# Strassen sums one at a time, attention at other points, and a softmax of ScalarE passes per head in a fused attention and two-layer kernel

## The chip, the cores and the metric

The kernel runs on one core of a Trainium2 chip. The metric is the device time of one execution in microseconds (us), as the median of several runs. TensorE (PE) multiplies, VectorE (DVE) and ScalarE (ACT) work on tiles, GpSimd (POOL) helps them, SyncE (SP) issues all DMAs in one queue.

## The reference

```python
# attention: B=4, H=8, S=768, D=64; chunks of 32 queries
for c in range(S // 32):
    k_full = concat([mem_k, k[:, :, c*32-16 : c*32+40]])       # 8 + 56 = 64 slots, cut at the ends
    scores = (1 / sqrt(D)) * q_c @ k_full.T
    scores = scores - max(scores, axis=-1)
    a = exp(scores)
    a = a / (sum(a, axis=-1) + 1e-9)
    out[c] = a @ v_full
x = out.transpose(0, 2, 1, 3).reshape(3072, 512)
# layer 1: 512 -> 2048 -> 512
r = maximum(x @ w_in, 0); y = (r * r) @ w_out
# layer 2: 512 -> 2048 -> 512, its own weights
h = y @ w_in2; out = (h * tanh(log1p(exp(h)))) @ w_out2
```

All of it is float32, and the result keeps float32 precision.

## The kernel before

**Steps.** The 3072 tokens are cut into three blocks of 1024, the 2048 hidden columns into eight chunks of 256. One step is one block and one chunk: steps 0 to 23 are layer 1, steps 24 to 47 layer 2, eight steps a block; behind step 47 follows a last stretch. In each step `product` (L478) makes the first matmul of its chunk, from two halves by two halves of both operands, with seven products where eight would be the plain way (Strassen in Winograd's form: S1 to S4 are sums of weight halves, T1 to T4 sums of halves of x). Each operand is split in a rounded part `hi` and a rest `lo`, so a product is six matmuls of 128x512. Results collect in banks a, b, c of PSUM: `u1` is a copy of the first product by ScalarE (L737), `u2`, `u3`, `c22`, `c21`, `c12` are additions on VectorE (L744 to L776), and `gate` (ACT) applies relu and square, or layer 2's function, and casts the result to `hi` (L491); GpSimd subtracts to get `lo` (`split_g`, L492).

**Second matmul.** Between the products of step s stands the second matmul of step s-1. In layer 1 it is eight `unit`s (L533), added to `y` by VectorE. In layer 2 it is seven `product2`s (L568) in pairs of banks 4-5 and 6-7, in the order of `PRODUCTS2`; VectorE adds each to its accumulator `m` (L556, 128x1024), or ScalarE copies it at the first chunk of a block (L579). When a block of layer 2 ends, `combine` adds the seven accumulators up to four outputs: four sums stand together behind the product of T2, three more behind the first three products of the next block's first step, and each output is then stored. The last stretch makes its four outputs in plain form (`last_unit`, L607), in pairs of banks.

**The written order.** The order of instructions on each engine is that of the program text. A step has 15 points, one behind each group of six matmuls (`rest`); at a point waiting stores are issued, one piece of the next weights is loaded, and work that was planned for it is done. `plan_attention` and `plan_w` put such work at offsets in points from a start:

```python
def at(s, i, *work):
    beside.setdefault((s + i // POINTS, i % POINTS), []).extend(work)
...
start, first, period = ((0, 4, 26), (NQ + 1, 10, 19))[sb]
```

**Attention.** It goes in pairs of 128-token tiles, twelve pairs, four for each block. Pairs 0 to 3 come ahead of step 0 (the head), pairs 4 to 7 lie in steps 0 to 7, pairs 8 to 11 in steps 9 to 14. In a pair, `scores` puts two halves of 128x512 in two banks (eight heads of 64 slots each in a half); `softmax` takes the maximum and subtracts it (DVE, L367, L368); `exps` is one exp over 128x512 for each half (ACT, L374); `normalize` sums (DVE, L378), adds 1e-9 and inverts (L380, L381) and multiplies (POOL, L384); `transpose_p` turns the probabilities on TensorE, `copy_pt` copies them to `pt` (ACT, L402), `values` multiplies by v (PE, L414, 128 small matmuls), `copy_x` copies to a stage (ACT, L426), `sums_x` makes T1 to T4 of x (POOL, in the head's last pair DVE), `store_x` stores them to DRAM. A later step loads and splits them again.

**Weights.** Weights come from DRAM in a form that a few passes restore: a rebias on ScalarE (L145), a decode on VectorE (L152), sums on VectorE, a cast to `hi` on ScalarE (L193, L211) and the rest on VectorE (L218); then they are stored to `w_d`, from which each step loads its part. Layer 2's entries are planned from step 8 on: six at one per step, ten more every 9 points from step 17.

**Buffers.** `spare` names the buffers in which the first three accumulators of a block lie (`xt0` to `xt2` or `raw0` to `raw2`, taking turns), while x of the next block is loaded into the others.

## Time and profile before

| | |
|---|---|
| median of 3 runs (lowest, highest) | 1168.34 us (1166.24, 1169.35) |
| the profiled execution: its own time, its span | 1169.24 us, 1167.2 us |
| busy: PE matmul, PE weight load | 1079.9 us (93%), 881.1 us (75%) |
| busy: DVE, ACT, POOL | 896.1 us (77%), 561.5 us (48%), 430.0 us (37%) |
| granted TensorE clock, mean | 0.972 of full speed |
| DMA over the span | 278 GB/s |

The span is the time between the first and the last instruction on the record; the execution's own time has 2 us around it. Busy shares are means over the whole span, over stages with different limits, so that a stretch that matters is read by itself. A clock of 1.00 is 2.4 GHz; a mean between says for how much of a stretch the half level, 1.2 GHz, was granted. A matmul's busy time includes what it takes longer at the half level. A row of a stretch gives its bounds and length, the busy us of PE, PEld, DVE, ACT and POOL in this order with the number of their instructions, the clock, the mean busy share of the DMA engines and what they moved. Steps are named by where their first `product` starts: step 0 at 62.24 us, step 15 at 468.4, step 17 at 509.2, step 26 at 705.8, the last stretch at 1125.2 with step 47 in it.

### The profile page before, as it was taken

To read this page: it belongs to the slowest core of one execution; us is meant where nothing else is said; L and a number is where in the kernel's file an instruction comes from. 1 tells how busy PE (TensorE), PEld (TensorE's weight loads), DVE (VectorE), ACT (ScalarE), POOL (GpSimd) and SP (SyncE) were. 2 spreads that over 40 slices of the span, in tenths; PEclk is the share of its full clock that TensorE was granted. 3 is DMA by queue.
4 is the path that set the end of the run, shared out by engine and by line. 5 is a ranking of instruction groups with operands and counts; after the bars stand their busy time and mean duration, and the time that the engine had idled before them with its cause. 6 is when DMAs were issued, how large, how long until landed. Compare 5 with 4: busy or idle time off the path is not lost.

```text
span 1167.2 us, 19779 instructions
## 1 busy us (share of the span) xinstructions
PE 1079.9 (93%) x7478; PEld 881.1 (75%) x7478; DVE 896.1 (77%) x1164; ACT 561.5 (48%) x879; POOL 430.0 (37%) x333
## 2 busy tenths in 40 slices
PE   6869899898799889999999999999989999799997
PEld 5748688776677778887777778888868888578885
DVE  5586879969666655678998677898878988768886
ACT  2467555555454444557565645444354443253331
POOL 2423223232223323223222244555355545245451
PEclk9999899999989889999999999999999999899998
DMA  9556867777998786869999958989997889867531
GB/s 359 231 193 233 293 214 262 260 277 248 384 320 315 263 292 241 280 237 395 342 338 329 362 218 289 314 304 339 345 309 276 303 304 391 277 207 230 161 128 72
DMA packets 192125, 324.94 MB, mean 278 GB/s; under 512 B 13344, under 2 KB 151072, under 8 KB 188192
## 3 DMA queue, kind: packets, MB, share of 16 engines
q1 hardware_dynamic: 192032, 323.69, 78.0%
q8 instruction: 60, 0.98, 0.3%
q14 instruction: 33, 0.27, 0.1%
HBM read 231.62 MB, written 92.01 MB: 277 GB/s over the span
## 4 chain that ended last, share of the span: by engine, by line
PE 56%; DVE 11%; DMA 7%; ACT 4%; issue 3%; SPq 0%; DVEq 0%; ACTq 0%
PE banks L478 26%; PE banks L568 17%; PE banks L533 10%; DMA w_d<-hi 2%; DVE m L556 2%; DVE y L547 1%; PE banks L414 1%; PE banks L607 1%; DMA w1s<-w_d 1%; DVE ty L632 1%; DVE val L152 1%; DVE r L519 1%; ACT r L497 1%; DMA xt<-xt_d 1%; DMA w2s<-w_d 1%
## 5 line engine op out<-in xcount | busy, mean ns | idle before, releaser
L478 PE MATMUL banks<-x,w1s 128*128 128x512 f32 x2016 | 507.8, 399 | 23.5 <-DVE u L763 7.5
L492 POOL TENSOR_TENSOR g<-r,g 128x512 fp32r<-128x512 f32 x206 | 287.3, 1401 | 537.5 <-ACT g L491 442.6
L478 PEld LDWEIGHTS banks<-x,w1s 128*128 128x128 f32 x2016 | 385.8, 193 | 112.5 <-DVE u L763 9.7
L533 PE MATMUL banks<-g,w2s 128*128 128x512 f32 x1152 | 282.4, 395 | 6.8 <-DVE y L547 5.3
L533 PEld LDWEIGHTS banks<-g,w2s 128*128 128x128 f32 x1152 | 217.2, 190 | 57.7 <-DVE y L547 8.2
L568 PE MATMUL banks<-g,w2s 128*128 128x512 f32 x966 | 241.3, 392 | 9.8 <-ACT m L579 7.6
L568 PEld LDWEIGHTS banks<-g,w2s 128*128 128x128 f32 x966 | 181.2, 189 | 52.2 <-ACT m L579 9.7
L556 DVE TENSOR_TENSOR m<-banks,m 128x1024 f32<-128x1024 f32 x144 | 173.6, 1218 | 34.9 <-PE banks L568 26.3
L491 ACT CAST g<-r 128x512 fp32r<-128x512 f32 x206 | 127.0, 621 | 37.5 <-DVE r L519 30.3
L547 DVE TENSOR_TENSOR y<-banks,y 128x512 f32<-128x512 f32 x168 | 112.0, 682 | 39.0 <-PE banks L533 38.9
L492 POOL TENSOR_TENSOR g<-more,g 128x512 fp32r<-128x512 f32 x55 | 79.7, 1453 | 81.0 <-ACT g L491 66.6
L497 ACT ACTIVATE r<-r 128x512 f32<-128x512 f32 x72 | 45.4, 631 | 69.7 <-DVE r L771 50.1
L501 ACT ACTIVATE r<-r 128x512 f32<-128x512 f32 x48 | 30.4, 632 | 71.4 <-DVE r L771 35.9
L211 ACT CAST hi<-val 128x1024 fp32r<-128x1024 f32 (+1 forms) x32 | 30.4, 949 | 69.5 <-DVE val L156 50.5
L498 ACT ACTIVATE r<-r 128x512 f32<-128x512 f32 x96 | 60.7, 632 | 3.1
L152 DVE TENSOR_SCALAR val<-val 128x512 f32<-128x512 f32 x64 | 38.9, 607 | 26.5 <-ACT val L145 26.4
L414 PE MATMUL banks<-pt,v 64*64 64x32 f32 x1536 | 39.9, 262 | 19.4 <-ACT pt L402 19.0
L218 DVE TENSOR_TENSOR val<-val,hi 128x1024 f32<-128x1024 f32 (+1 forms) x32 | 37.2, 1162 | 25.2 <-ACT hi L211 25.0
L414 PEld LDWEIGHTS banks<-pt,v 64*64 64x64 f32 x1536 | 37.0, 185 | 25.7 <-ACT pt L402 24.8
L737 ACT COPY u<-banks 128x512 f32<-128x512 f32 x48 | 28.1, 585 | 52.0 <-PE banks L478 52.0
L384 POOL TENSOR_TENSOR p<-p,sum 128x512 f32<-128x512 f32 x24 | 28.7, 1215 | 63.3 <-DVE sum L381 25.0
L344 PE MATMUL banks<-k,q 64*32 64x64 f32 x1536 | 37.5, 250 | 13.2 <-DMA k<-k_dram 7.1
(71 smaller groups left out, 999.9 us busy)
## 6 DMA issues: line engine op xcount, KB each, us to landing
w1s<-w_d SPq DMA_DIRECT2D x280, 256.0 KB, 5.4
w2s<-w_d SPq DMA_DIRECT2D x229, 256.0 KB, 5.3
raw<-w_dram SPq DMA_DIRECT2D x64, 512.0 KB, 5.0
w_d<-w1s SPq DMA_DIRECT2D x8, 1792.0 KB, 7.5
x<-xs_d SPq DMA_DIRECT2D x14, 1024.0 KB, 10.7
k<-k_dram SPq DMA_DIRECT2D x24, 512.0 KB, 7.0
v<-v_dram SPq DMA_DIRECT2D x24, 512.0 KB, 8.9
xt<-xt_d SPq DMA_DIRECT2D x21, 512.0 KB, 7.3
```

Source lines behind the costliest of these rows:

```text
L152: nc.vector.tensor_scalar(out=val, in0=val, scalar1=LIMIT, scalar2=-LIMIT * NEGATIVE, op0=ALU.min, op1=ALU.max)
L344: nc.tensor.matmul(out=s4[32 * c:32 * c + 32, j, hp, :], lhsT=q_t[p][r0:r0 + 64, j, hp, 32 * c:32 * c + 32], rhs=k_t[p][r0:r0 + 64, j, hp, ...
L414: nc.tensor.matmul(out=x_ps[par][64 * h2:64 * h2 + 64, o:o + 32], lhsT=v_t[p][j][r0:r0 + 64, h2, a, c, :], rhs=pt_t[p][r0:r0 + 64, h2, j, ...
L478: nc.tensor.matmul(out=ps, lhsT=w[:, a, f:f + 128], rhs=x[:, xi, c, kk, :], start=start and i == 0, stop=stop and i == len(order) - 1, ski ...
L491: nc.scalar.copy(out=g[:, 0], in_=r)
L492: nc.gpsimd.tensor_tensor(out=g[:, 1], in0=r, in1=g[:, 0].bitcast(FP32), op=ALU.subtract)
L497: nc.scalar.activation(out=r, in_=h, func=ACTF.Relu)
L498: nc.scalar.activation(out=r, in_=r, func=ACTF.Square)
L533: nc.tensor.matmul(out=ps, lhsT=w[:, a, blk(f), d % 2 * 128:d % 2 * 128 + 128], rhs=g_t[s, (f, t)][:, c, :], start=i == 0, stop=i == len(o ...
L547: nc.vector.tensor_tensor(out=y, in0=ps, in1=y, op=ALU.add)
L556: engine.tensor_tensor(out=to, in0=in0, in1=in1, op=ALU.add)
L568: nc.tensor.matmul(out=bank(first + d), lhsT=w[:, a, 128 * d:128 * d + 128], rhs=g[:, c, :], start=i == 0, stop=i == 2)
```

## The change

Four things are changed.

1. **Softmax in the steps.** For pairs 4 to 11 VectorE still takes the maximum, then makes `mneg`, the maximum times minus the scale (128x8). ScalarE makes, from PSUM, one exp for each head (64 columns, eight for each half), with `mneg` as bias and the sum of the row as a second result (L389 of the kernel after). The subtraction and the sum on VectorE are left out. Pairs 0 to 3 keep the old form.
2. **Points.** The two halves' exps stand at offsets 3 and 4, the later parts of a pair one or two points later; pairs 4 to 7 come every 25 points where it was 26, pairs 8 to 11 start two points earlier. Layer 2's weights come as seven entries from step 8 on, then nine every 10 points.
3. **Block sums.** `SUMS` lists the seven sums one at a time; each stands behind a product of its own: one behind T2, one behind T1 (these two products change places), one early in the next step, four behind that step's first products. `spare` gives the last block's accumulators `raw0` to `raw2`; `last_unit` uses banks 0 to 3 first.
4. **Head.** In the head the last normalisation and the sums of pair 2 go to VectorE, and four `place_x` calls (which split x into hi and lo) stand earlier.

```diff
@@ -39,10 +39,12 @@
 PRODUCTS = [(A11, B11), (S2, T2), (S1, T1), (A12, B21), (S3, T3), (A22, T4), (S4, B22)]
-PRODUCTS2 = [(A11, B11), (S4, B22), (A12, B21), (S3, T3), (S1, T1), (S2, T2), (A22, T4)]
+PRODUCTS2 = [(A11, B11), (S4, B22), (A12, B21), (S3, T3), (S2, T2), (S1, T1), (A22, T4)]
 STEPS = 2 * NSB * NQ
 OUTPUTS = {T4: (1, 0), B21: (0, 0), T1: (1, 1), B22: (0, 1)}
+SUMS = [(T2, B11), (T3, T2), (T2, T1), (T1, T3), (T4, T3), (B22, T2), (B21, B11)]
@@ -276,7 +278,7 @@
     def spare(sb, i):
-        return f"{('xt', 'raw')[sb % NSB % 2]}{i % 3}"
+        return f"{('xt', 'raw')[(sb - NSB) % 2]}{i % 3}"
@@ -357,31 +359,48 @@
                         )
+    m_neg = {}
     def softmax(p, h2):
         if h2 == 0:
             p_t[p] = pool.tile([128, 2, 8, SLOTS], FP32, tag=f"g{2 + p % 2}" if early(p) else "xt0", name="p")
             r_t[p] = sp.tile([128, 2, 8], FP32, tag="sum", name="sum")
+        s8 = s_ps[p, h2].rearrange("p (a s) -> p a s", a=8)
+        mx = sp.tile([128, 8], FP32, tag="mx", name="mx")
+        nc.vector.tensor_reduce(out=mx, in_=s8, axis=AX.X, op=ALU.max)
+        if early(p):
+            nc.vector.tensor_tensor(
+                out=p_t[p][:, h2], in0=s8, in1=mx.unsqueeze(2).to_broadcast([128, 8, SLOTS]), op=ALU.subtract
+            )
+        else:
+            m_neg[p, h2] = sp.tile([128, 8], FP32, tag="mneg", name="mneg")
+            nc.vector.tensor_scalar(out=m_neg[p, h2], in0=mx, scalar1=-scale, scalar2=None, op0=ALU.mult)
+    def exps(p, h2):
         pr = p_t[p][:, h2]
         s8 = s_ps.pop((p, h2)).rearrange("p (a s) -> p a s", a=8)
-        mx = sp.tile([128, 8], FP32, tag="mx", name="mx")
-        nc.vector.tensor_reduce(out=mx, in_=s8, axis=AX.X, op=ALU.max)
-        nc.vector.tensor_tensor(
-            out=pr, in0=s8, in1=mx.unsqueeze(2).to_broadcast([128, 8, SLOTS]), op=ALU.subtract
-        )
-    def exps(p, h2):
-        pr = p_t[p][:, h2]
-        nc.scalar.activation(out=pr, in_=pr, func=ACTF.Exp, scale=scale)
-    def normalize(p):
-        for h2 in range(2):
-            nc.vector.tensor_reduce(out=r_t[p][:, h2], in_=p_t[p][:, h2], axis=AX.X, op=ALU.add)
+        if early(p):
+            nc.scalar.activation(out=pr, in_=pr, func=ACTF.Exp, scale=scale)
+            return
+        m = m_neg.pop((p, h2))
+        for i in range(8):
+            nc.scalar.activation(
+                out=pr[:, i], in_=s8[:, i], func=ACTF.Exp, scale=scale, bias=m[:, i:i + 1],
+                accum_out=r_t[p][:, h2, i:i + 1],
+            )
+    def normalize(p, engine=nc.gpsimd):
+        if early(p):
+            for h2 in range(2):
+                nc.vector.tensor_reduce(out=r_t[p][:, h2], in_=p_t[p][:, h2], axis=AX.X, op=ALU.add)
         r = r_t[p]
         nc.vector.tensor_scalar_add(out=r, in0=r, scalar1=1.0e-9)
         nc.vector.reciprocal(out=r, in_=r)
         for h2 in range(2):
             pr = p_t[p][:, h2]
-            nc.gpsimd.tensor_tensor(
+            engine.tensor_tensor(
@@ -581,25 +600,19 @@
         add(m, ps, m)
-    def combine(sb, blk, store):
+    def combine(sb, to, other, store=False):
         m = {b: m_t[sb, b] for _, b in PRODUCTS2}
-        if blk == T2:
-            add(m[T2], m[T2], m[B11])
-            add(m[T3], m[T3], m[T2])
-            add(m[T2], m[T2], m[T1])
-            add(m[T1], m[T1], m[T3])
-        else:
-            add(m[blk], m[blk], m[{T4: T3, B22: T2, B21: B11}[blk]])
-        if store:
-            store_y(sb, *OUTPUTS[T1 if blk == T2 else blk], m[T1 if blk == T2 else blk])
+        add(m[to], m[to], m[other])
+        if store and (to, other) in SUMS[3:]:
+            store_y(sb, *OUTPUTS[to], m[to])
     def last_unit(s, n):
         sb = where(s)[1]
         blk = list(OUTPUTS)[n]
         i, t = OUTPUTS[blk]
-        first = (4 + 2 * (pairs[0] % 2), 4 + 2 * ((pairs[0] + 1) % 2), 0, 2)[n]
+        first = (0, 2, 4 + 2 * (pairs[0] % 2), 4 + 2 * ((pairs[0] + 1) % 2))[n]
@@ -645,14 +658,15 @@
             2: lambda: softmax(p, 1),
-            3: lambda: (exps(p, 0), exps(p, 1), load_k(p + 1) if (p + 1) % PSB else None),
-            5: lambda: (normalize(p), load_v(p) if p > PSB else None),
-            11: lambda: transpose_p(p),
-            12: lambda: copy_pt(p),
-            14: lambda: (values(p), load_q(p + 1) if (p + 1) % PSB else None),
-            15: lambda: copy_x(p),
-            16: lambda: sums_x(p, nc.gpsimd),
-            20: lambda: store_x(p),
+            3: lambda: (exps(p, 0), load_k(p + 1) if (p + 1) % PSB else None),
+            4: lambda: exps(p, 1),
+            6: lambda: (normalize(p), load_v(p) if p > PSB else None),
+            12: lambda: transpose_p(p),
+            13: lambda: (copy_pt(p), load_q(p + 1) if (p + 1) % PSB else None),
+            16: lambda: values(p),
+            17: lambda: copy_x(p),
+            18: lambda: sums_x(p, nc.gpsimd),
+            22: lambda: store_x(p),
@@ -720,14 +734,16 @@
             _, sb, j = where(s - 1)
-            final = s == STEPS - 1
-            if (j == NQ - 1 or final) and PRODUCTS2[i][1] == T2:
-                combine(sb, T2, not final)
-            if final and PRODUCTS2[i][1] == T4:
-                for blk in (T4, B22, B21):
-                    combine(sb, blk, False)
-            if sb > NSB and j == 0 and i < 3:
-                combine(sb - 1, (T4, B22, B21)[i], True)
+            blk = PRODUCTS2[i][1]
+            if s == STEPS - 1:
+                for n in {T2: (0,), T1: (1, 2, 3), T4: (4, 6, 5)}.get(blk, ()):
+                    combine(sb, *SUMS[n])
+            elif j == NQ - 1:
+                for n in {T2: (0,), T1: (1,)}.get(blk, ()):
+                    combine(sb, *SUMS[n])
+            elif sb > NSB and j == 0:
+                for n in {B11: (3,), B22: (4,), B21: (5,), T3: (6,)}.get(blk, ()):
+                    combine(sb - 1, *SUMS[n], store=True)
@@ -738,6 +754,8 @@
                 split_g(s - 1, T3, r_ff[s - 1, T3])
+                if where(s - 1)[1] > NSB and where(s - 1)[2] == 0:
+                    combine(where(s - 1)[1] - 1, *SUMS[2])
@@ -814,10 +832,14 @@
             copy_pt(p)
-        def multiply(p):
+        def multiply(p, *others):
             values(p)
+            for other in others:
+                place_x(*other)
             copy_x(p)
-            sums_x(p, nc.vector if p == PSB - 1 else nc.gpsimd)
+            if p == PSB - 1:
+                place_x(p, 0, 3)
+            sums_x(p, nc.vector if p >= PSB - 2 else nc.gpsimd)
@@ -844,16 +866,11 @@
         place_x(0, 3, 7)
-        normalize(3)
+        normalize(3, nc.vector)
         turn(2)
         multiply(2)
-        place_x(1, 0, 3)
-        place_x(1, 3, 7)
         turn(3)
-        multiply(3)
-        place_x(2, 0, 3)
-        place_x(2, 3, 7)
-        place_x(3, 0, 3)
+        multiply(3, (1, 0, 3), (1, 3, 7), (2, 0, 3), (2, 3, 7))
@@ -868,20 +885,22 @@
         for n, e in enumerate(seconds):
-            if n < NQ - 2:
+            if n < NQ - 1:
                 plan_w(NQ + n, 0, e, "Aa|D|d|RS|s|L||||r|l", lambda e, i: round_w2(e, i, "xt2"), split_w2, "val")
             else:
-                n -= NQ - 2
+                n -= NQ - 1
                 hi = (["xt0", "xt1"], ["xt2", "at1"])[n % 2]
                 plan_w(
-                    2 * NQ + 1, 9 * n, e, "Aa|D|d|RS|s|Lr||l",
+                    2 * NQ + 1, 10 * n, e, "Aa|D|d|RS|s|Lr||l",
                     lambda e, i, hi=hi: round_w2(e, i, hi[i]), split_w2, ("val", "at0")[n % 2],
                 )
         for sb in range(NSB - 1):
             p = PSB * (sb + 1)
-            start, first, period = ((0, 4, 26), (NQ + 1, 10, 19))[sb]
-            at(start, 0, *([lambda p=p: load_k(p)] if sb else []), lambda p=p: load_q(p))
+            start, first, period = ((0, 4, 25), (NQ + 1, 8, 19))[sb]
+            at(start, 0, lambda p=p: load_q(p))
+            if sb:
+                at(start, 0, lambda p=p: load_k(p))
```

ScalarE around step 11, from the last gates of step 10 to step 11's `u1`: `pt` is what the product of pair 9 needs, `hi` a weight cast, r and g the gate, `stage` pair 8's x, `u_3965` step 11's `u1`. Before:

```order
L211 CAST hi<-val 128x1024
L497 ACTIVATE r<-r 128x512
L498 ACTIVATE r<-r 128x512
L491 CAST g<-r 128x512
L402 COPY pt<-banks 128x512 x2
L497 ACTIVATE r<-r 128x512
L498 ACTIVATE r<-r 128x512
L491 CAST g<-r 128x512
L426 COPY stage<-banks 128x4x128 x2
L145 ACTIVATE val<-raw 128x512 x2
L737 COPY u_3965<-banks 128x512
```

After (the lines' numbers are those of the kernel after, `u_4049` is the `u1`):

```order
L213 CAST hi<-val 128x1024
L421 COPY pt<-banks 128x512 x2
L516 ACTIVATE r<-r 128x512
L517 ACTIVATE r<-r 128x512
L510 CAST g<-r 128x512
L516 ACTIVATE r<-r 128x512
L517 ACTIVATE r<-r 128x512
L510 CAST g<-r 128x512
L445 COPY stage<-banks 128x4x128 x2
L147 ACTIVATE val<-raw 128x512 x2
L753 COPY u_4049<-banks 128x512
```

The copies of `pt` stood behind the cast and a whole gate; now they follow the cast, ahead of both gates.

VectorE at the first block change of layer 2, from the last addition of step 32 (`r<-banks`) to `u3` of step 33 (`u_7925`); `m<-m` are the sums of `combine`, `u_7855` is `u2`, r and more are the gate's parts. Before:

```order
L776 TENSOR_TENSOR r<-banks,u_7700 128x512
L556 TENSOR_TENSOR m<-banks,m 128x1024
L556 TENSOR_TENSOR m<-m 128x1024 x4
L556 TENSOR_TENSOR m<-banks,m 128x1024
L519 TENSOR_TENSOR r<-r 128x512
L519 TENSOR_TENSOR r<-r,more 128x512
L519 TENSOR_TENSOR r<-r 128x512
L744 TENSOR_TENSOR u_7855<-banks,u_7841 128x512
L519 TENSOR_TENSOR r<-r 128x512
L556 TENSOR_TENSOR m<-m 128x1024 x3
L763 TENSOR_TENSOR u_7925<-banks,u_7841 128x512
```

After (`u_7965` is `u2`, `u_8035` is `u3`; the first of the seven sums stands two rows above the first row here):

```order
L794 TENSOR_TENSOR r<-banks,u_7812 128x512
L575 TENSOR_TENSOR m<-banks,m 128x1024
L575 TENSOR_TENSOR m<-m 128x1024
L575 TENSOR_TENSOR m<-banks,m 128x1024
L538 TENSOR_TENSOR r<-r 128x512
L538 TENSOR_TENSOR r<-r,more 128x512
L538 TENSOR_TENSOR r<-r 128x512
L575 TENSOR_TENSOR m<-m 128x1024
L762 TENSOR_TENSOR u_7965<-banks,u_7950 128x512
L538 TENSOR_TENSOR r<-r 128x512
L575 TENSOR_TENSOR m<-m 128x1024 x3
L781 TENSOR_TENSOR u_8035<-banks,u_7950 128x512
```

The group of four sums is spread: one behind each of two products, one ahead of `u2`, and three, as before, ahead of `u3`.

ScalarE between steps 3 and 4, where pair 6's exps stand ahead of step 4's `u1` (`u_1947`). Before:

```order
L497 ACTIVATE r<-r 128x512
L498 ACTIVATE r<-r 128x512
L491 CAST g<-r 128x512
L374 ACTIVATE p<-p 128x512 x2
L145 ACTIVATE val<-raw 128x512 x2
L737 COPY u_1947<-banks 128x512
L193 CAST w1s<-val 128x768
```

After (`u_1998` is the `u1`):

```order
L516 ACTIVATE r<-r 128x512
L517 ACTIVATE r<-r 128x512
L510 CAST g<-r 128x512
L389 ACTIVATE p,sum<-banks,mneg 128x64 x16
L147 ACTIVATE val<-raw 128x512 x2
L753 COPY u_1998<-banks 128x512
L195 CAST w1s<-val 128x768
```

In the place of two passes stand sixteen, each with a second result, and the same instructions follow them.

## Rows read from the trace of the kernel before

**Rows 1.** Busy time of each engine by stretch, granted clock, DMA share, GB/s

```profile
62.20:468.40 406.20, 369.37 (x3495) 299.17 (x3496) 297.05 (x461) 215.06 (x343) 124.48 (x108) 0.95 0.76 271
468.40:509.20 40.80, 40.80 (x182) 33.78 (x181) 26.16 (x33) 23.18 (x35) 10.31 (x9) 1.00 0.72 249
509.20:705.80 196.60, 187.47 (x806) 150.95 (x805) 162.65 (x242) 113.34 (x172) 54.20 (x39) 0.99 0.91 329
359.10:389.20 30.10, 26.58 (x231) 22.19 (x227) 17.93 (x31) 14.21 (x23) 8.76 (x8) 0.89 0.83 296
705.80:840.10 134.30, 133.99 (x589) 110.03 (x588) 115.31 (x118) 58.30 (x92) 70.31 (x49) 1.00 0.91 325
840.10:865.80 25.70, 21.69 (x85) 16.62 (x84) 21.41 (x20) 12.70 (x18) 11.73 (x7) 0.93 0.74 244
1000.20:1030.00 29.80, 21.98 (x86) 17.02 (x85) 18.11 (x19) 12.85 (x18) 9.35 (x7) 0.89 0.71 235
1125.20:1167.20 42.00, 33.24 (x133) 26.32 (x131) 30.99 (x29) 7.87 (x13) 11.11 (x8) 0.92 0.13 50
```

**Rows 2.** TensorE's timeline: start, us, line, tiles, count, idle time before and releaser

```profile
62.24 7.20 PE L478 MATMUL banks<-x,w1s 128*128 128x512 f32 x18 [3.57 <-ACT x L446]
...
140.63 4.12 PE L414 MATMUL banks<-pt,v 64*64 64x32 f32 x128 [3.25 <-ACT pt L402]
...
382.81 4.12 PE L414 MATMUL banks<-pt,v 64*64 64x32 f32 x128 [3.45 <-ACT pt L402]
...
858.62 4.50 PE L478 MATMUL banks<-x,w1s 128*128 128x512 f32 x12 [3.17 <-DVE u L763]
...
1015.89 2.93 PE L568 MATMUL banks<-g,w2s 128*128 128x512 f32 x6 [6.36 <-ACT m L579]
...
1151.24 11.04 PE L607 MATMUL banks<-g,w2s 128*128 128x512 f32 x36 [3.84 <-DVE m L556]
```

**Rows 3.** Groups by line: count, busy us, mean ns, idle before and releasers

```profile
L374 ACT ACTIVATE p<-p 128x512 f32<-128x512 f32 x24 | 14.8, 629 | 31.5 <-DVE p L368 31.5
L579 ACT COPY m<-banks 128x1024 f32<-128x1024 f32 x21 | 20.9, 1012 | 11.5 <-DVE m L556 6.4 <-DMA out_dram<-m 2.9 <-PE banks L568 2.1
L737 ACT COPY u<-banks 128x512 f32<-128x512 f32 x48 | 28.1, 585 | 52.0 <-PE banks L478 52.0
L368 DVE TENSOR_TENSOR p<-banks,mx 128x512 f32<-128x512 f32 x24 | 16.6, 692 | 2.2 <-PE banks L344 0.8 <-DVE mx L367 0.2
L378 DVE TENSOR_REDUCE sum<-p 128x8 f32<-128x512 f32 x24 | 15.4, 677 | 1.9 <-ACT p L374 1.7
L380 DVE TENSOR_SCALAR sum<-sum 128x16 f32<-128x16 f32 x12 | 2.4, 196 | 0.4
```

**Rows 4.** Timelines of TensorE and of ScalarE at the start of step 4

```profile
170.52 4.24 PE L478 MATMUL banks<-x,w1s 128*128 128x512 f32 x18
...
172.93 0.58 ACT L737 COPY u<-banks 128x512 f32<-128x512 f32 x1
```

**Rows 5.** ScalarE's timeline in steps 11 and 13

```profile
377.39 1.05 ACT L211 CAST hi<-val 128x1024 fp32r<-128x1024 f32 x1 [3.20 <-DMA w_d<-hi]
...
382.18 1.07 ACT L402 COPY pt<-banks 128x512 f32<-128x512 f32 x2
...
418.31 1.22 ACT L145 ACTIVATE val<-raw 128x512 f32<-128x512 f32 x2 [5.85 <-DMA w_d<-val]
```

**Rows 6.** Timelines of VectorE and of GpSimd at the first block change

```profile
840.22 5.01 DVE L556 TENSOR_TENSOR m<-m 128x1024 f32<-128x1024 f32 x4
...
851.22 6.74 DVE L556 TENSOR_TENSOR m<-m 128x1024 f32<-128x1024 f32 x3
...
847.74 4.71 POOL L492 TENSOR_TENSOR g<-r,g 128x512 fp32r<-128x512 f32 x3 [7.98 <-ACT g L491]
```

**Rows 7.** ScalarE's timeline at the second block change

```profile
1019.28 1.01 ACT L579 COPY m<-banks 128x1024 f32<-128x1024 f32 x1 [2.92 <-DMA out_dram<-m]
```

**Rows 8.** VectorE's timeline, its last addition

```profile
1162.32 1.23 DVE L556 TENSOR_TENSOR m<-banks,m 128x1024 f32<-128x1024 f32 x1 [1.49 <-PE banks L607]
```

## The prediction

> **What bounds the kernel now.** I read the stretches by engine first [rows 1]. TensorE sets the time: in steps 26 to 32 it is busy for 133.99 of 134.30 us, 19.19 us a step, and in steps 15 and 16 for 40.80 of 40.80, 20.40 us a step. So a change pays only where TensorE stands idle, or works at the half level of its clock (1.2 GHz) behind an idle stretch. The other rows of the group show where that is: steps 0 to 14 take 406.2 us at a mean clock of 0.95; steps 17 to 25 take 196.6 us where eight steps at 20.40 and one at 19.19 make 182.4, so 14 us too many; the steps in which layer 2 passes from one token block to the next take 25.7 and 29.8 us, 6.5 and 10.6 too many; and the last stretch takes 42.0 us. Then I read TensorE's timeline for what ended each wait [rows 2]: the start of layer 1 waits for a cast of x (3.57 us), three attention products wait for the transposed probabilities `pt` (3.25 and 3.45 us; the third row, at 420 us, is like them), the two block changes wait 3.17 for `u3` on VectorE and 6.36 for a copy of ScalarE, the end waits 3.84 for VectorE. The 128 matmuls of a product that waited take 4.12 us, at the half clock: in the step of the second of them (359 to 389 us) the mean clock is 0.89, so that of 30.1 us some 6.6 us ran at half speed [rows 1], which lose 3.3 us of work on top of the wait.
>
> **The change, part by part.** Times are against the profiled execution, 1169.24 us with a span of 1167.2; the median of the runs, 1168.34, is 0.9 lower.
>
> *Softmax, prices.* Per head half VectorE loses the subtraction (692 ns) and the sum (677) and gains one 128x8 multiply, for which the 128x16 scalar row stands, 196 [rows 3]. That is 1.17 us less, sixteen times, 18.8 us. ScalarE does eight passes over 64 columns, each with a sum as second result, for one pass over 512 of 629 ns. No row shows such a pass. Below: copies from PSUM take 585 ns for 512 columns and 1012 for 1024 [rows 3], so 0.83 ns a column and 158 fixed, 211 ns for 64. Above: as much as the whole 512 pass, 629. I take the middle, 0.42, as if the sum were a second small instruction: 3.4 us a half, 6.7 a pair against 1.26, so 5.5 more per pair and 44 us for eight. ScalarE is busy for 215 of 406 us there [rows 1], so most of it has room; what counts is what stands behind the passes in ScalarE's queue. The small VectorE work of `normalize` now waits for the last pass, and that holds VectorE up about as long as the dropped sums took: I count no gain for VectorE, except in steps 5 and 6, where the passes follow `gate` in ScalarE's idle middle.
>
> The Trainium skill, "ScalarE: Activation LUTs", section "What ACT_TABLE_LOAD costs", speaks against cutting the pass: a pass with a per-partition bias costs about 280 ns plus 0.833 a column, and neighbours overlap by 93, which is an estimated 240 ns a pass and 1.9 us a half. It gives no price for the sum; with 240 ns the two losses (c) and (f) below vanish and the total falls by 3.5 us; no row shows the pass itself.
>
> (a) Head: the last pair's normalisation and pair 2's block sums leave GpSimd for VectorE, and three casts move ahead of the last stage copy, so layer 1's first product starts some 2 us before its 62.24 [rows 2]; but the sums of pair 3 now follow one more cast, and in step 0 the sixteen passes (6.7 us) delay the next use of VectorE. Net 0.8 gained, from 3 lost to 3.5 gained.
> (b) Step 2: the product comes one group of 1.36 us (20.40/15) later behind its copies, so the wait of 3.25 falls to 1.9, and some half-clock time with it: 3 us, from 1.4 to 4.6.
> (c) Pair 6: its sixteen passes end step 3's queue, ahead of the rebias passes and of step 4's `u1`, which starts at 172.93 where its step starts at 170.52 [rows 4], 2.4 us in. 5.5 us later it is at 7.9; the fourth product needs its bank at 6.8. Lost 1.5, from 0 to 5.
> (d) Steps 5 and 6: 2.4 us less of VectorE work in two steps that are full of it: 3 gained, from 0 to 4.7. (e) Step 7 waits for the x that pair 7 stores; its sums stand one point earlier: 1.5, from 0 to 3.5.
> (f) Pair 8: as (c), ahead of step 10's `u1` and of three copies of `y`: lost 2, from 6 lost to 1 gained.
> (g) Step 11: pair 9 moves two points forward, its product keeps its place. In ScalarE's queue `pt` stood behind a whole gate, at 382.18 [rows 5]; now it follows the cast at 377.39, so it is there at about 379.5 and the wait of 3.45 all but ends. 6.6 with the clock; I take 5, since that cast itself waited 3.20 for a store. From 1 to 6.6.
> (h) Step 13: the copies of pair 10 stood behind a rebias pass that waited 5.85 us for a store [rows 5]; now they are queued a step earlier, ahead of it. 6.5 with the clock, I take 5, from 1 to 6.6.
> (i) Steps 17 to 25: one of ten weight entries goes to step 14, which has room, and the others come every 10 points, not 9. VectorE loses some 8 us there (three passes for each half, the sums, two splits), but three casts, where it was two, now fall just ahead of a `u1`. 2 gained, from 3 lost to 6 gained.
> (j) First block change. Before, four sums follow each other behind one product (5.01 us) and three more (6.74) stand ahead of `u3` [rows 6]. Now one follows each of two products, one stands ahead of `u2` and three ahead of `u3`. VectorE reaches the next step some 4 us earlier. How long a sum takes depends on its neighbour: 1.25 us where GpSimd stood idle, 2.25 beside GpSimd's splits, which themselves took 1.57. With 1.25 each nothing waits, and 6.5 is gained; with 2.25, `u3` is ready about 1.4 us earlier only. I take 4, from 1.4 to 6.5.
> (k) Second change: besides, the outputs of the last block go to `raw`, not to `xt`, from which the block before is still being stored: the copy at 1019.28 waited 2.92 us for that store [rows 7]. 10.6 at most, 5.5 at least (it becomes as long as the other change less 1.4); I take 8.
> (l) End: the first two of the four last products use banks 0 to 3, which nothing holds, so the wait of 3.84 [rows 2] and its half clock go: 48 matmuls at 0.228 (19.19/84) are done some 7 us sooner. The sums and additions on VectorE are then late next: its last addition, which ended at 1163.55 (1162.32 plus 1.23) [rows 8], ends 5 to 6 us earlier. 5.5, from 3.8 to 6.
>
> The swap of two products needs the split of T2 a product earlier; in the clean steps it stands ready, and I count nothing (a miss would cost one split, 1.6 us, in each block change). The stores of (k) move on SP's queue with their sums; weights wait behind them there, but are loaded a step ahead: nothing. The loads of k, v and q move by a point or two; nothing, with the bounds of (f) as cover.
>
> Sum: 0.8+3-1.5+3+1.5-2+5+5+2+4+8+5.5 = 34.3, so 1134.9 for this execution and 1134 for the median. The terms' half ranges, taken as independent, make 10 us, so this case alone lies between 1122 and 1146.
>
> **The rivals.** *The passes cost 0.63 us.* 3.4 us more per pair; wholly on the path in pairs 6 and 8, half so in 4 and 5: 10 us, and pairs 9 and 10 lose the half of (g) and (h): 1149. For: the sum may be a slow second instruction. Against: no ScalarE row has more than some 0.2 us fixed.
> *The stalls of steps 11 and 13 come back.* They hang on stores of 5.85 and 3.20 us in a stretch whose DMA share is 0.83 [rows 1]; a faster TensorE asks for more. (b), (g) and (h) go: 1147.
> *The sums stay slow.* A sum took 2.25 us beside GpSimd's splits against 1.25 without [rows 6]. Here all seven may fall beside splits in both changes; then `u3` is late again, and (j) and (k) keep their low ends, 1.4 and 5.5: 1139. The Trainium skill, "SBUF — State Buffer", section "Who interferes with whom", makes this the rule: a VectorE instruction with two SBUF inputs and a GpSimd one that reads SBUF exclude each other for a whole instruction; by that rule every sum beside a split is slow, and the two prices in the rows agree with it.
> *Slower.* Every pair's passes lie on the path: a gate, `u1` or `pt` stands behind them and TensorE waits for all of it. At 0.42 that is 44 us for eight pairs against 37.8 of gains without (c) and (f): 1174. It decides from 0.41 us a pass on. For: pairs 6 and 8. Against: ScalarE's 191 idle us in that stretch, and four pairs whose passes precede a gate that waits for VectorE anyway.
>
> **How the numbers follow.** Forecast 0.59, dear passes 0.12, stalls that return 0.14, slow sums 0.08, slower 0.07. The low end, 1118, is the forecast's with half of its (a), (g), (h) and (j) at their best; the high end takes in the first three rivals and a mix of them: 1153. A measurement tells 0.3% (3.5 us) from no change: slower takes 0.06 of its rival, no change 0.03 between the two sides, and faster the rest, 0.91.
>
> **What would show it.** Right: no wait of TensorE over 1 us at the last products and at the second block change; `pt` not the releaser in steps 11 and 13; passes of 0.4 us apart; `u1` late in steps 4 and 10. Wrong: passes of 0.6 us or more, steps 0 to 14 no shorter than 400 us in sum, or a block change still above 24 us.

## The result and the profile after

The changed kernel takes 1127.3 us (median of 4 runs, 1126.7 to 1130.86), the kernel before 1167.29 beside it; the ratio is 0.9662, with an interval of 0.9636 to 0.9688. Forecast were 1134, between 1118 and 1153. The profiled execution took 1127.79 us, with a span of 1126.0 against 1167.2.

The stretches by engine, after, in the columns of [rows 1]: steps 0 to 14, steps 17 to 25, the first block change, the last stretch:

```profile
61.40:453.50 392.10, 361.82 (x3495) 294.17 (x3496) 285.38 (x459) 244.00 (x585) 124.98 (x107) 0.96 0.80 285
495.80:680.30 184.50, 183.10 (x805) 150.62 (x804) 156.34 (x230) 110.78 (x168) 54.85 (x39) 1.00 0.93 334
814.70:836.90 22.20, 19.67 (x86) 15.62 (x85) 19.55 (x18) 12.26 (x18) 11.56 (x8) 1.00 0.63 213
1088.50:1126.00 37.50, 30.06 (x133) 24.57 (x131) 31.23 (x29) 7.76 (x13) 12.07 (x8) 0.96 0.15 56
```

Steps 0 to 14 took 406.2 us and take 392.1; steps 17 to 25 took 196.6 and take 184.5, which is eight times 20.40 and 19.19 plus 2; the block changes fell from 25.7 and 29.8 to 22.2 and 22.1, the end from 42.0 to 37.5. ScalarE is busy for 244 us in the first stretch, where it was 215, and VectorE for 285, where it was 297.

By the terms of the prediction, in us, from the starts of the steps in the traces; the last column is a second profile of the changed kernel, from the runs below:

| stretch | terms | forecast | after | second profile |
|---|---|---|---|---|
| head, step 0 | (a) | -0.8 | -1.7 | -1.2 |
| steps 1 to 4 | (b), (c) | -1.5 | -1.9 | -4.0 |
| steps 5 to 8 | (d), (e) | -4.5 | -3.8 | -3.1 |
| steps 9 to 16 | (f), (g), (h) | -8.0 | -5.9 | -0.3 |
| steps 17 to 25 | (i) | -2.0 | -12.1 | -12.6 |
| step 33 | (j) | -4.0 | -3.5 | -2.2 |
| step 41 | (k) | -8.0 | -7.7 | -6.3 |
| last stretch | (l) | -5.5 | -4.5 | -4.5 |
| span | | -34.3 | -41.2 | -34.3 |

One profile is a weak measure of steps 9 to 14: in the four profiles (of the kernel before and of three runs below) whose code there is that of before, they take 165.9 to 173.0 us. The profile of before, at 173.0, is the longest of the four.

TensorE's waits after, as in [rows 2] (two products of attention, the two block changes, the end):

```profile
135.21 0.30 PE L433 MATMUL banks<-pt,v 64*64 64x32 f32 x2 [1.48 <-ACT pt L421]
...
180.36 0.30 PE L433 MATMUL banks<-pt,v 64*64 64x32 f32 x2 [1.40 <-ACT pt L421]
...
830.96 3.02 PE L497 MATMUL banks<-x,w1s 128*128 128x512 f32 x12 [2.53 <-DVE u L781]
...
987.41 3.02 PE L497 MATMUL banks<-x,w1s 128*128 128x512 f32 x12 [2.50 <-DVE u L781]
1107.52 11.04 PE L620 MATMUL banks<-g,w2s 128*128 128x512 f32 x48
```

No attention product waits over 1.5 us for `pt`, ScalarE's copy at the second block change is no releaser any more, and the 48 matmuls at the end follow without a wait. `u3` is what both block changes still wait for.

A pass of the new softmax and the start of the next, in ScalarE's timeline of step 0 (sixteen follow each other):

```profile
76.99 0.31 ACT L389 ACTIVATE p<-banks,mneg 128x64 f32<-128x64 f32 x1
77.20 0.19 ACT L389 ACTIVATION_READ_ACCUMULATOR p<-banks,mneg 128x1 f32 x1
77.29 0.30 ACT L389 ACTIVATE p<-banks,mneg 128x64 f32<-128x64 f32 x1
```

It is two instructions, the exp and a read of the sum, which overlap: the next pass starts 0.29 to 0.30 us after the last, sixteen take 4.7 us. I had put 0.42 a pass.

### The profile page after: what moved, and what is told of

The parts are those of the page before. It is cut to its first block, busy times and chain, and to the rows that moved or that the text cites. A ratio compares the mean times of both kernels' runs of the same rounds, so it can differ in the third digit from the quotient of the medians.

```text
span 1126.0 us, 19983 instructions
## 1 busy us (share of the span) xinstructions
PE 1061.0 (94%) x7478; PEld 871.6 (77%) x7478; DVE 884.1 (79%) x1154; ACT 589.1 (52%) x1119; POOL 429.0 (38%) x327
## 4 chain that ended last, share of the span: by engine, by line
PE 70%; DVE 12%; ACT 6%; DMA 6%; issue 5%; POOL 1%; SPq 0%; DVEq 0%; ACTq 0%; POOLq 0%
PE banks L497 31%; PE banks L587 17%; PE banks L552 16%; DVE m L575 3%; PE banks L433 3%; PE banks L346 2%; DMA w_d<-hi 2%; ACT p L389 1%; DVE r L538 1%; DMA k<-k_dram 1%; ACT r L517 1%; DMA xt<-xt_d 1%; ACT r L516 1%; DVE y L566 1%; DVE ty L645 1%
## 5 line engine op out<-in xcount | busy, mean ns | idle before, releaser
L497 PE MATMUL banks<-x,w1s 128*128 128x512 f32 x2016 | 500.9, 395 | 21.7 <-DVE u L781 8.7
L497 PEld LDWEIGHTS banks<-x,w1s 128*128 128x128 f32 x2016 | 380.4, 190 | 107.4 <-DVE u L781 10.4
L346 PEld LDWEIGHTS banks<-k,q 64*32 64x32 f32 x1536 | 32.7, 122 | 24.1 <-issue 20.6
L158 DVE SCALAR_TENSOR_TENSOR val<-raw,val 128x512 uint32<-128x512 uint32 x64 | 49.0, 765 | 2.2
L403 POOL TENSOR_TENSOR p<-p,sum 128x512 f32<-128x512 f32 x22 | 25.9, 1197 | 58.8 <-DVE sum L400 39.4
```

The costliest lines, as they stand in the source:

```text
L158: nc.vector.scalar_tensor_tensor(out=vb, in0=low, scalar=29, in1=vb, op0=ALU.logical_shift_right, op1=ALU.bitwise_or)
L346: nc.tensor.matmul(out=s4[32 * c:32 * c + 32, j, hp, :], lhsT=q_t[p][r0:r0 + 64, j, hp, 32 * c:32 * c + 32], rhs=k_t[p][r0:r0 + 64, j, hp, ...
L497: nc.tensor.matmul(out=ps, lhsT=w[:, a, f:f + 128], rhs=x[:, xi, c, kk, :], start=start and i == 0, stop=stop and i == len(order) - 1, ski ...
```

## The experiments

The steps are compared by their starts in the profiles; ratios are to the kernel before on the same chip, whose median was 1164.9, 1163.9 and 1164.2 us in the three sets.

**One part of the change alone.** Four kernels are the kernel before with one part each; the fourth part of the change, the head, was not run alone.

```diff
+SUMS, PRODUCTS2, combine, done, last_unit, spare and the early sum as in the change
```

> The kernel before with the block sums one at a time, the swapped products, the other order of banks at the end and the last block's accumulators in raw; attention, softmax, weights and head as before. My theory, that the terms add: step 33 falls by 3.5 us, step 41 by 7.7, the last stretch by 4.5, the rest stays, so 15.7 us in all: about 1151.6 us. Rival, that these stretches gained because the steps before them came at other times: less than half of it, 1160 or above.

Measured: 0.9861 (0.9833 to 0.989), 1149.96 us. Step 33 fell by 2.2, step 41 by 6.4, the end by 4.5: 13.1 of the 21 us by which the profile is shorter; 7 more lie in steps 9 to 14, which this edit doesn't touch. So these terms add, and the 7 us lie within the spread of steps 9 to 14.

```diff
-            if n < NQ - 2:
+            if n < NQ - 1:
-                n -= NQ - 2
+                n -= NQ - 1
-                    2 * NQ + 1, 9 * n, e, "Aa|D|d|RS|s|Lr||l",
+                    2 * NQ + 1, 10 * n, e, "Aa|D|d|RS|s|Lr||l",
```

> The kernel before with only the plan of layer 2's weights changed: seven entries from step 8, then nine every 10 points from step 17. Theory of phases: at a period of 9 points the fourth and the ninth entry put a cast that waits for VectorE at the first point of a step, ahead of u1; at 10 no entry does it so late, and steps 17 to 25 fall by 12 us: about 1155.3. Rival, that half of those 12 us comes from attention work that now ends earlier: steps 17 to 25 fall by 4 to 7 us, 1161 to 1163. Rival, that the entry that moves to step 14 costs there what it saves: 1165 or above.

Measured: 0.9875 (0.9848 to 0.9902), 1152.03 us; steps 17 to 25 fell by 11.6, steps 19 to 24 to 20.4 each. The theory came right and the two rivals fall: the weights alone give what (i) gained.

```diff
+softmax and exps as in the change (normalize without the sums), both halves at offset 3
```

> The kernel before with only the softmax of pairs 4 to 11 as passes per head, at the old points (both halves at offset 3). Theory, that the softmax alone is worth little: a pass takes 0.29 us where I put 0.42, sixteen 4.7 us where two took 1.26; VectorE is relieved of 18.8 us but is not what the stalls of steps 11 and 13 wait for: steps 1 to 14 fall by 0 to 5 us, 1162 to 1167. Rival, that it brings most of the gain of steps 1 to 14: 10 us or more, 1157 or below. Rival, that it loses time at old points, because the passes delay u1: 1170 or above.

Measured: 1.0037 (1.0013 to 1.0061), 1168.37 us: a little slower than before. My expectation missed: steps 1 to 4 lose 4.0, steps 5 to 8 gain 3.2, steps 9 to 14 lose 4.3. The loss of step 4 (29.4 us where it was 24.6) can be read in order of time, ScalarE first, then TensorE:

```profile
169.57 0.31 ACT L387 ACTIVATE p<-banks,mneg 128x64 f32<-128x64 f32 x1
...
174.22 1.31 ACT L145 ACTIVATE val<-raw 128x512 f32<-128x512 f32 x2
175.34 0.67 ACT L754 COPY u<-banks 128x512 f32<-128x512 f32 x1
...
188.36 0.30 PE L431 MATMUL banks<-pt,v 64*64 64x32 f32 x2 [2.04 <-ACT pt L419]
```

The step starts at 170.15. Sixteen passes end at 174.2; behind them stand the rebias passes, which give VectorE its work, and `u1`, 5.2 us into the step where it was 2.4 [rows 4]. What is late next is not the fourth product, as (c) had it, but `pt` at the other end of the step: TensorE waits 2.04 and then works at the half level (the step's mean clock is 0.88).

```diff
+plan_attention's offsets, start, first, period and the first loads as in the change
```

> The kernel before with only attention's points and periods changed, the softmax in its old form. Theory, that the points bring the gain of steps 1 to 14 by taking pt out from behind a gate and a rebias pass: step 11 falls by 6 us, step 13 by 5, steps 1 to 14 in sum by 8 to 13: 1154 to 1159. Rival, that the points pay only with VectorE relieved of the subtraction and the sums: less than 4 us, 1163 or above.

Measured: 0.9874 (0.9833 to 0.9916), 1152.59 us: step 11 falls by 6.2, step 13 by 2.9, steps 1 to 14 by 14.6, a little more than expected. The points bring it, with the old softmax; but half of it, 7.4, lies in steps 1 to 3, which the theory did not name, and steps 9 and 10 take 3.3 us more than before. Sums, weights and points together make 1.4 + 1.25 + 1.3 = 3.9%, the softmax takes 0.4 back, and the change, with the head in it, measures 3.4, in the next set 2.8: the parts nearly add.

**What the softmax is worth in the changed kernel.** Four kernels on one chip.

> The changed kernel once more, beside the next three on the same chip. Both theories: a ratio to the kernel before of 0.962 to 0.970, and a step 4 of some 30 us (24.6 before), a step 5 of some 22.4 (25.0 before).

Measured, unchanged: 0.9716 (0.969 to 0.9741), 1130.63 us, a little out of what was expected. Step 4 took 26.8, not 30: the same wait for `pt` (1.41) was there, but the clock stayed at 1.00.

```diff
-        if early(p):
+        if True:
```

(in `softmax`, `exps` and `normalize`)

> The changed kernel with the softmax of pairs 4 to 11 back in its old form (subtraction, one exp per half, sum on VectorE), all else as changed. My theory, that the passes per head lose more ahead of u1 in steps 4 and 10 than they save on VectorE: step 4 falls from 30 to 24.6 us, step 5 rises to 24.5, step 6 to 24.7, and the kernel is 1 to 5 us faster than the changed one. Rival, that the new points need the passes: 3 us or more slower than the changed one, with waits for pt in steps 11 and 13 again.

Measured: 0.9709 (0.9686 to 0.9732), 1130.13 us: no difference. Step 4 is 25.2, step 5 24.5, step 6 24.7 as expected, but the rival falls too: step 11 is 23.5 as in the change, and no product waits for `pt` over 2 us. The passes give back in step 4 what VectorE gains behind it.

```diff
-        if early(p):
+        if early(p) or p in (4, 6, 8):
```

> The changed kernel with the old softmax for pairs 4, 6 and 8 alone, whose passes stand ahead of a u1 or late in a step; pairs 5, 7, 9, 10 and 11 keep their passes. My theory, that the place of the passes decides: step 4 falls to 24.6 us, step 5 stays between 22.4 and 24.5, and the kernel is 3 to 6 us faster than the changed one, and not slower than that with the old softmax. Rival, that what VectorE saves in steps 4 and 5 is worth as much as the passes cost there: within 2 us of the changed one.

Measured: 0.9655 (0.9632 to 0.9679), 1123.86 us, 6.8 us below the changed kernel beside it, a little more than expected. Step 4 is 24.9, step 5 23.3, step 6 23.5; steps 9 and 10 take 65.8 together, 68.3 and 71.0 in the two profiles of the change. Another 4.3 us against the second of these lie in step 13, which took 26.8 in the first profile of the change too: they are not shown to be this edit's.

```diff
-            3: lambda: (exps(p, 0), load_k(p + 1) if (p + 1) % PSB else None),
-            4: lambda: exps(p, 1),
-            6: lambda: (normalize(p), load_v(p) if p > PSB else None),
+            (7 if p == 6 else 3): lambda: (exps(p, 0), load_k(p + 1) if (p + 1) % PSB else None),
+            (8 if p == 6 else 4): lambda: exps(p, 1),
+            (9 if p == 6 else 6): lambda: (normalize(p), load_v(p) if p > PSB else None),
```

> The changed kernel with pair 6's sixteen passes four points later, behind step 4's u1 and not ahead of it, and its normalisation three points later. My theory, that step 4 loses its 5 us because the passes hold u1 and the rebias passes back 2.4 us or more, and with them VectorE and pt: step 4 falls to between 24.6 and 27 us and step 5 keeps its 22.4; 3 to 5 us faster than the changed one. Rival, that the passes cost the same wherever they stand in step 4, for the gate and pt stand behind them there too: step 4 stays at 29 us or more.

Measured: 0.9669 (0.9645 to 0.9693), 1125.75 us, 4.9 below the changed kernel. Step 4 falls to 24.0 and step 5 is 23.3. The same sixteen passes, behind `u1`, cost nothing: their place was the price. The edit moves `normalize` too, so that what `u1` costs by being late and what `normalize` costs by holding VectorE up are not told apart. How the passes held VectorE up is seen in VectorE's timeline of the changed kernel, and ScalarE's:

```profile
166.48 1.30 ACT L147 ACTIVATE val<-raw 128x512 f32<-128x512 f32 x2
167.59 0.66 ACT L753 COPY u<-banks 128x512 f32<-128x512 f32 x1
...
166.71 0.18 DVE L399 TENSOR_SCALAR sum<-sum 128x16 f32<-128x16 f32 x1 [4.27 <-ACT p L389]
```

`normalize` on VectorE waits 4.27 us for the last pass, in a step that starts at 161.30, with all of VectorE's work behind it.

**Why steps 17 to 25 gained 12 us and not 2.**

```diff
-                    2 * NQ + 1, 9 * n, e, "Aa|D|d|RS|s|Lr||l",
+                    2 * NQ + 1, 9 * n, e, "Aa|D|d||RS|s|Lr||l" if n % 5 == 3 else "Aa|D|d|RS|s|Lr||l",
```

> The kernel before, in which the first cast and the sum with it of the fourth and the ninth of the ten entries stand one point later; on ScalarE that changes places of this cast and of u1 in steps 19 and 22, and nothing else. Theory of place: these two casts wait some 4 us for a decode on VectorE and hold u1 up, so steps 19 and 22 fall by 2.5 and 4.2 us to 20.4, and the other steps from 17 to 25 stay: 6 to 8 us faster in that stretch. Rival, that VectorE has too much to do there, and u1 late is only the sign of it: steps 19 and 22 stay above 22 us.

Measured: 0.9995 (0.9975 to 1.0016). My theory falls as an account of the whole: steps 19 and 22 fell to 21.5 and 22.2, but steps 18, 20 and 23 rose to 22.1, 22.2 and 22.3, and the stretch gained 0.3. The wait for ScalarE's `u1` became waits for VectorE's `u2` and `u3` and for late weights. The edit puts all later passes of those two entries one point later, not that cast and sum alone, and no run tells which of them the other steps pay for.

```diff
-            if n < NQ - 2:
+            if n < NQ - 1:
-                n -= NQ - 2
+                n -= NQ - 1
```

> The kernel before with seven entries from step 8 and nine from step 17, still every 9 points. Theory of place: the fourth and the ninth of the nine keep the bad place, so steps 19 and 22 stay at 22 to 25 us; only the work of one entry goes, from steps 23 to 25: steps 17 to 25 fall by 2 to 5 us. Rival, that fewer entries are what helped: 9 us or more.

Measured: 0.998 (0.9963 to 0.9996); steps 17 to 25 fell by 3.1, step 22 stayed at 24.8 as expected, step 19 fell to 20.9 against expectation. So 3 of the 11.6 us are the entry that went to step 14, and the other 8.4 the tenth point.

Steps 18 to 22, busy time by engine, of the kernel before, of the weights alone, and of nine entries every 9 points, with its step 22 by itself:

```profile
529.57:641.90 112.33, 105.97 (x452) 84.83 (x450) 102.39 (x165) 66.17 (x103) 28.31 (x20) 0.98 0.96 349
```

```profile
525.97:629.02 103.05, 102.26 (x451) 84.38 (x450) 97.62 (x154) 63.28 (x98) 28.51 (x20) 1.00 0.99 358
```

```profile
526.96:638.43 111.47, 105.39 (x452) 85.08 (x450) 97.26 (x156) 66.44 (x103) 29.42 (x22) 0.98 0.96 347
613.67:638.43 24.76, 22.32 (x92) 17.98 (x90) 16.64 (x27) 13.78 (x22) 6.99 (x6) 0.93 0.82 288
```

Five clean steps of TensorE are 102.0 us, and VectorE had 102.4 us of work in the five steps of before, so that it looks like the bound. The third row speaks against this: with nine entries VectorE's work is 97.26 at every 9 points and 97.62 at every 10, and yet the five steps take 111.5 and 103.1 us. In step 22 of the 9 points VectorE is busy for 16.6 of 24.8 us, and there the wait is the one that the theory of place named, on ScalarE and then on TensorE:

```profile
621.50 1.04 ACT L211 CAST hi<-val 128x1024 fp32r<-128x1024 f32 x1 [3.93 <-DVE val L156]
...
623.08 4.61 PE L478 MATMUL banks<-x,w1s 128*128 128x512 f32 x12 [2.44 <-ACT u L737]
```

So the amount of VectorE's work in these steps does not decide. Where in a step the passes fall does, or how closely the entries follow each other; no run separates the two. At 10 points three casts still stand just ahead of a `u1`, in steps 18, 20 and 22, but in the profile of the weights alone they wait only 0.76 to 2.33 us for VectorE, `u1` starts 4.3 to 5.7 us into its step, where it was 8.5 in steps 19 and 22 of before, and no wait for `u1` is left. Why moving the bad casts by one point alone gained nothing, while moving all entries did, stays open.

**The second block change.**

```diff
-        return f"{('xt', 'raw')[sb % NSB % 2]}{i % 3}"
+        return f"{('xt', 'raw')[(sb - NSB) % 2]}{i % 3}"
```

> The kernel before with the last block's accumulators in raw, all else as before. Theory, that step 41 lost 2.9 us and the clock behind it to the store of xt, the rest to the order of the sums: step 41 falls from 29.8 to about 25.7 us, as long as step 33; 3 to 5 us in all. Rival, that the sums on VectorE hold the same copy up anyway: step 41 falls by less than 1.5 us.

Measured: 0.9961 (0.9945 to 0.9977), 1158.63 us; step 41 falls by 5.4 to 24.4, and no wait for the store is left. So of the 6.4 to 7.7 us of (k) most is this one line, with the clock that it brings back (1.00 in that step, where it was 0.89).

**A faster version.**

```diff
+pair 6's passes as in the run with later passes
-        if early(p):
+        if early(p) or p == 8:
```

> The changed kernel with pair 6's passes behind step 4's u1, as in the run with later passes, and pair 8's softmax in the old form; pairs 4, 5, 7, 9, 10 and 11 keep their passes in their places. My theory: steps 1 to 8 as in the run with later passes, steps 9 to 14 as in the run with some pairs: a ratio to the kernel before of 0.960 to 0.966, 4 to 7 us faster than the changed kernel. Rival, that pair 8's form makes no difference: 0.966 to 0.970.

Measured: 0.9622 (0.9603 to 0.9641), 1119.68 us beside 1164.21 of before: the lowest time of all. It was not timed beside the changed kernel, whose ratio was 0.9662 on one chip and 0.9716 on another, so that it lies 0.4 to 1.0% below that by the ratios; against the run with some pairs (0.9655) the intervals overlap. Steps 9 to 14 are 9.8 us shorter than before, as with some pairs.

## Why the prediction was right, and where not

**The frame** was right: time lay where TensorE stood idle and not in clean steps, which stayed as they were. No rival took place as a whole: the range held, and the forecast lay 6.7 us above the result. Of the signs, the last products run without a wait, `pt` is no releaser in steps 11 and 13, and `u1` is late in steps 4 and 10 (6.3 and 6.5 us into the step); but passes are 0.29 us apart and not 0.4, and the second block change still waits 2.50 us, for `u3`.

That the sum came so near is in part luck, for errors cancelled: in the first profile (i) gained 10 us more than forecast and (b) 4.5 more, while (c) came out 4.1 worse, (f) 2.6, (e) 1.8, and (j), (k) and (l) 1.9 together. The second profile fell by the forecast 34.3 with terms that were as far off.

**(j), (k), (l)** came out at 3.5, 7.7 and 4.5 for 4, 8 and 5.5, and run alone at 2.2, 6.4 and 4.5. The third rival is half true: in step 33 a sum beside GpSimd's splits takes 1.75 to 2.32 us, and 1.21 behind them, and `u3` makes TensorE wait 2.53 where it was 3.17. The step gained more than that difference. With the points alone, the old sums and the same wait of 3.17, step 33 took 24.4 us at a clock of 1.00, where before it took 25.7 at 0.93: so 1.3 of the 3.5 us go with the clock, and 2.2 with the sums, as in the run of the sums alone. That what is more than the shorter wait comes from the four sums that no longer stand together at the step's start is argued, not shown. The sums agree with the rule of the Trainium skill, "SBUF — State Buffer", section "Who interferes with whom", that a VectorE instruction with two inputs in SBUF and a GpSimd one that reads SBUF exclude each other.

**(b)** was too small: steps 1 to 3 fell by 7.5 and 6.2 us in the two profiles, by 7.4 with the points alone, where 3 was forecast and 4.6 the bound. The product's wait for `pt` became 1.48 us, near the 1.9 that was expected; the rest is in the clock, whose mean was 0.92 and 0.90 in steps 2 and 3 of before and is 1.00 and 0.94 after, and in smaller waits that went.

**(g)** was right: step 11 fell by 6.6, 6.2 with the points alone. **(h)** holds in part. Step 13 fell by 5.2 in one profile of the changed kernel and by 1.0 in the other. Its rebias pass still waits for a store, 1.61 us and 3.01, and now the copy of x stands behind it, for which the next scores wait; in the second profile, ScalarE and then TensorE:

```profile
412.21 1.23 ACT L147 ACTIVATE val<-raw 128x512 f32<-128x512 f32 x2 [3.01 <-DMA w_d<-val]
...
418.04 0.81 PE L346 MATMUL banks<-k,q 64*32 64x64 f32 x43 [2.31 <-ACT stage L445]
```

That is the second rival in small: the store's wait, which was `pt`'s, is now `stage`'s.

**The softmax prices.** 0.42 us a pass was too much; it measured 0.29. The estimate of 0.24 without the sum, worked out from the Trainium skill, "ScalarE: Activation LUTs", section "What ACT_TABLE_LOAD costs", was nearer than my middle; that (c) and (f) vanish at such a price did not come out. They were right that the passes are dear ahead of `u1`, but too small, and (c) had the wrong path. In step 4 TensorE waits 1.00 us for `u2`, which needs `u1`, and 1.40 for `pt`, not for the fourth product's bank; the step lost 5.6 us in the first profile, with a stretch at the half clock, and 2.2 in the second, where (c) had 1.5. Steps 9 and 10 lost 4.6 and 7.3 where (f) had 2, and 3.3 of this comes with the points alone, which no term had. (d) was right: steps 5 and 6 gained 4.2 and 3.3 for 3, and softmax alone gives 3.2 us back in steps 5 to 8. The sign of the sum of both is open to within 0.3%: the old form is as fast. In the rival of passes that all lie on the path a number is wrong: by its own terms, eight pairs at sixteen passes less 1.26 us against 37.8, it decides from 0.37 us a pass and not from 0.41; the measured 0.29 is below both.

**(e)** failed: step 7 still waits 2.3 to 2.4 us for `u3`, where it waited 2.07 before, and gained nothing.

**(i)** is the term that was mis-sized: 2 for 12.1, with 6 as its bound. I counted two casts ahead of a `u1` before and three after, and set them as a loss against VectorE's 8 us of work. The traces have three in both, in steps 19, 21 and 22 of before and in steps 18, 20 and 22 after. What differs is how long they wait for VectorE: 2.34 us at most after, where TensorE doesn't wait for `u1`, and 3.94 in steps 19 and 22 of before, where it does; ScalarE and TensorE in step 19 of before:

```profile
558.78 0.83 ACT L211 CAST hi<-val 128x768 fp32r<-128x768 f32 x1 [3.94 <-DVE val L156]
...
560.15 3.01 PE L478 MATMUL banks<-x,w1s 128*128 128x512 f32 x12 [2.21 <-ACT u L737]
```

That this alone is the price is not shown, for the run with the cast later gained nothing. The entry that left gave 3.1 us, and the tenth point, whose casts I had priced as a loss, 8.4. The rows for it are those of each step that was too long; I had read nine steps in one, clean ones with them [rows 1].

It also stays open what TensorE's scores of steps 9 and 10 wait for: 2.8 to 3.5 us stand as "issue" in the profiles of the changed kernel, and no run here tried it. In step 9 the kernel before had such a wait too (3.54); in step 10 it is new, and shorter (1.5 to 2.3) where pair 8 has the old softmax.

## What to carry to other kernels

Where work is planned beside the bottleneck's at a fixed period, the period is worth a run of its own: the same nine entries cost 8.4 us more every 9 points than every 10. Moving one late instruction alone moved the wait to other steps. An engine's sum of busy time doesn't show that it is the bound: two runs with the same sum took 111.5 and 103.1 us. When passes are moved from one engine to another, ask what stands behind them in the new queue before asking what they cost: the same sixteen passes cost 2 to 6 us ahead of a copy and nothing behind it. Test the parts of a change apart, for one that adds nothing can hide behind others that do.

## What the runs showed of the hardware

The same wait is followed by different clocks from one execution to the next. In step 33 TensorE waited 2.53 us for `u3` in both profiles of the changed kernel; in the first the next twelve matmuls took 3.02 us, in the second, at a mean clock of 0.93 in that step, 4.51:

```profile
835.17 4.51 PE L497 MATMUL banks<-x,w1s 128*128 128x512 f32 x12 [2.53 <-DVE u L781]
```

So a step with such a wait is 22.2 or 23.5 us long, and step 4 30.2 or 26.8, with nothing else changed. It is not the chip: of the four kernels timed together, which are alike from layer 2 on, two have 22.2 us in step 33 and two 23.5, all behind a wait of 2.53. And in a row of passes with a sum each, the exp's own duration grows from 0.31 to 0.40 us over the sixteen while the distance from one to the next stays at 0.29.
